# Attention and a dense layer on one core: query loads ahead of key copies, masks on VectorE

## The chip, the cores and the metric

The kernel runs on one core of a Trainium2 chip. A core has TensorE (matmuls; PE in the profile), VectorE (DVE), ScalarE (ACT), GpSimd (POOL) and SyncE (SP), each with a queue of instructions that it works off in order, and 16 DMA engines between HBM and the on-chip memory. DMAs are issued from the queues of SyncE and of POOL. The metric is device time of one execution in microseconds.

## The reference

Block-sparse attention, then a dense layer; 4 batches, 8 heads, 768 tokens, head size 64, blocks of 32 tokens:

```python
mask = np.abs(blk_i - blk_j) <= 1
mask = mask | (blk_i == 0) | (blk_j == 0) | (blk_i == n_blocks - 1) | (blk_j == n_blocks - 1)
for qb in range(n_blocks):
    for kb in sampled_blocks[qb]:                 # three random blocks for each query block
        mask[qb*32:(qb+1)*32, kb*32:(kb+1)*32] = True
scores = np.where(mask, scale * q @ k.T, -1e9)
attn = exp(scores - max) / (sum + 1e-9)
x = (attn @ v)                                    # to 3072 tokens x 512
h = x @ w_in                                      # 512 x 2048, weights given as float64
g = s * relu(h)**2 + b
return g @ w_out
```

Which blocks are sampled is known only at run time.

## The kernel before, in words

Attention is cut into slots. Four dense slots in each half of the batches handle the first and last query block, which see all keys. A sparse slot handles one query block of two batches: 256 score columns, made of window blocks, global blocks and three sampled blocks. There are 44 sparse slots; here they are counted from 0, so that slots 0, 1 and 2 are the first of three streams and use the query tiles qr_4s, qr_0s and qr_3s, one tile for four slots of a stream. Order at the start: four dense slots (qr_0d), then the sparse slots of the first half.

One sparse slot is this work. POOL copies its window keys and global keys out of the key tile kt into kk (lines 880 and 882), the last block (891), and three sampled blocks (893), whose numbers it holds in registers. TensorE makes the scores from kk and the query tile (943). VectorE adds the mask mt and takes the maximum (960), ScalarE takes the exponential (972), TensorE transposes (1000), VectorE and ScalarE copy the result to pt (1011, 1013), TensorE multiplies with window values vA and sampled values vB (1052), VectorE scales (1058), TensorE transposes back (1064), ScalarE copies (1069), SyncE spills to xd (1076). TensorE takes these in a written-out order: scores of slot i+2, value product of slot i, transposes of slot i+1, transposes back of slot i, scores of slot i+3, and so on. Sampled keys are held for four slots and sampled values for five, so POOL copies for a slot when the scores four slots before are done, and SyncE loads sampled values up to five slots ahead. Window values go into one of three rows of vA, free when the product three slots before is done.

At the start SyncE loads the sampled list (795), the keys of the first half in eight pieces (692), the first dense queries (706), global values (758, 760), window values (771) and, with registers that it loads from the tile packed (837), sampled values (865). VectorE makes packed from the list (801 and the helper line 100). POOL makes constants, then `sparse_sampled`, a chain of 17 small instructions that writes the mask mt (helper line 100), then loads the registers (837), then works on queries (706) and key copies.

Behind attention 256 us into the execution comes the dense layer, which TensorE fills nearly to the end; its weights are loaded and split during attention.

A planner sets the order on each engine: every operation has an engine, a cost, a priority (a due time in units of TensorE's work, smaller is earlier), and what it depends on (`deps`), follows (`order`, the start of another operation) or allocates. The planner issues the earliest startable operation in order of priority. The engines keep the order that comes out; on the chip only semaphores hold them. DMAs take turns in eight lanes for each issuing queue, so a DMA waits until the one eight before it has landed.

## Time and profile before

| | us |
|---|---|
| median of 3 runs (780.3 to 783.9) | 780.48 |
| profiled execution | 780.98 |
| its span | 779.2 |
| TensorE busy | 735.6 (94%) |
| VectorE busy | 579.0 (74%) |
| ScalarE busy | 472.1 (61%) |
| POOL busy | 240.1 (31%) |
| TensorE busy, 0 to 20 us | 16.43 |
| TensorE busy, 30 to 40 us | 6.34 |

The page has a row of busy time for each engine, the span in 40 slices, the DMA queues, the chain of work that ended last, and groups of instructions. The trace also answers with a timeline of one engine, with waits, and with the busy time in a given stretch. In a row of the timeline the first number is the start, the second the length, x the count, and in brackets stands the idle time before it with what ended it. "Issue" is time in which the engine waited for nothing that the profile shows; a register load is such time. Lines are those of the kernel before.

### The profile page before, as it was taken

To read this page: it belongs to the slowest core of one execution; us is meant where nothing else is said; L and a number is where in the kernel's file an instruction comes from. 1 tells how busy PE (TensorE), PEld (TensorE's weight loads), DVE (VectorE), ACT (ScalarE), POOL (GpSimd) and SP (SyncE) were. 2 spreads that over 40 slices of the span, in tenths; PEclk is the share of its full clock that TensorE was granted. 3 is DMA by queue.
4 is the path that set the end of the run, shared out by engine and by line. 5 is a ranking of instruction groups with operands and counts; after the bars stand their busy time and mean duration, and the time that the engine had idled before them with its cause. 6 is when DMAs were issued, how large, how long until landed. Compare 5 with 4: busy or idle time off the path is not lost.

```text
span 779.2 us, 21332 instructions
## 1 busy us (share of the span) xinstructions
PE 735.6 (94%) x8032; PEld 619.8 (80%) x8032; DVE 579.0 (74%) x1441; ACT 472.1 (61%) x1141; POOL 240.1 (31%) x390
## 2 busy tenths in 40 slices
PE   8799798988798999999889999999999999999997
PEld 6377675566576998998778899988888888988996
DVE  4657477878687699999897688687678678666652
ACT  4657475977687677778864344465544467445443
POOL 4746243524320232221022223222322233222321
PEclk9989999999899999999999999999999999999999
DMA  9988988856774544544623321225000022000002
GB/s 242 217 211 227 235 227 236 197 146 186 191 203 130 149 135 137 165 156 128 141 108 95 89 75 68 68 63 135 0 1 2 1 61 82 1 1 0 2 1 81
DMA packets 101110, 89.41 MB, mean 115 GB/s; under 512 B 50192, under 2 KB 79504, under 8 KB 101008
## 3 DMA queue, kind: packets, MB, share of 16 engines
q1 hardware_dynamic: 98704, 81.76, 38.2%
q0 software_dynamic: 2304, 6.29, 3.4%
q8 instruction: 63, 1.03, 0.6%
q14 instruction: 39, 0.32, 0.1%
HBM read 69.15 MB, written 14.68 MB: 108 GB/s over the span
## 4 chain that ended last, share of the span: by engine, by line
PE 79%; DVE 7%; ACT 4%; issue 4%; DMA 3%; POOL 1%; SPq 1%; POOLq 0%; ACTq 0%; DVEq 0%
PE m L611 19%; PE o L475 10%; PE o L476 10%; PE o L474 10%; PE s L943 6%; PE xs L1052 6%; PE t L1000 5%; PE h L432 3%; PE h L434 3%; PE h L433 3%; PE od L1042 2%; PE xs L1064 1%; DMA qr_3s<-in_q_dup_dram 1%; DMA xd<-xst 1%; DVE xp L595 1%
## 5 line engine op out<-in xcount | busy, mean ns | idle before, releaser
L453 POOL TENSOR_TENSOR hid<-hid,hid 128x384 fp32r<-128x384 f32 x120 | 132.3, 1103 | 400.5 <-ACT hid L629 249.0
L628 ACT ACTIVATE hid<-hid,sb_b,sb_s 128x384 f32<-128x384 f32 x96 | 68.0, 709 | 151.8 <-DVE hid L622 151.8
L972 ACT ACTIVATE ptile<-ptile,nm 128x256 f32<-128x256 f32 (+1 forms) x208 | 107.3, 518 | 43.2 <-DVE nm L960 42.8
L960 DVE CUSTOM_DVE_ANT_1 ptile<-s,mt 128x256 f32<-128x256 f32 x176 | 64.4, 421 | 34.7 <-PE s L943 33.6
L476 PE MATMUL o<-woutr,hid 128*128 128x512 f32 x168 | 66.5, 396 | 0.0
L475 PE MATMUL o<-woutr,hid 128*128 128x512 f32 x168 | 66.3, 395 | 0.0
L611 PE MATMUL m<-wout,win 128*128 128x384 f32 x264 | 62.7, 340 | 3.6 <-ACT hid L437 1.9
L474 PE MATMUL o<-woutr,hid 128*128 128x512 f32 x168 | 65.3, 389 | 0.0
L611 PE MATMUL m<-xp,wop 128*128 128x384 f32 x288 | 58.3, 337 | 0.0
L475 PE MATMUL o<-win,hid 128*128 128x512 f32 x144 | 56.8, 394 | 0.0
L622 DVE SCALAR_TENSOR_TENSOR hid<-hid 128x384 f32<-128x384 f32 x96 | 54.3, 566 | 3.3
L1052 PEld LDWEIGHTS xs<-vA,pt 128*32 128x32 f32 x1696 | 36.1, 113 | 26.0 <-issue 8.7
L611 PE MATMUL m<-xp,win 128*128 128x384 f32 x288 | 55.1, 338 | 1.4 <-DVE xp L595 0.7
L1000 PE MATMUL t<-ident,ptile 128*128 128x128 f32 x352 | 51.4, 289 | 3.6 <-issue 3.5
L611 PEld LDWEIGHTS m<-xp,win 128*128 128x128 f32 x288 | 51.0, 188 | 4.6 <-DVE xp L595 1.2
L1052 PE MATMUL xs<-vA,pt 128*32 128x64 f32 x1696 | 48.5, 228 | 6.2 <-issue 5.6
L629 ACT CAST hid<-hid 128x384 fp32r<-128x384 f32 x96 | 49.4, 515 | 7.2
L611 PEld LDWEIGHTS m<-xp,wop 128*128 128x128 f32 x288 | 51.5, 188 | 2.1
L611 PEld LDWEIGHTS m<-wout,win 128*128 128x128 f32 x264 | 47.3, 188 | 6.9 <-ACT hid L437 2.8
L882 POOL COPY kk<-kt 128x256 f32<-128x256 f32 (+2 forms) x46 | 20.5, 449 | 103.3 <-PE s L943 103.3
L476 PE MATMUL o<-win,hid 128*128 128x512 f32 x126 | 49.8, 395 | 0.0
L474 PE MATMUL o<-win,hid 128*128 128x512 f32 x126 | 49.2, 390 | 0.2
(187 smaller groups left out, 1843.3 us busy)
## 6 DMA issues: line engine op xcount, KB each, us to landing
vB<-in_v_dram SPq DMA_DIRECT2D x109, 128.0 KB, 3.9
vA<-in_v_dram SPq DMA_DIRECT2D x72, 128.0 KB, 4.1
raw_o<-in_w_out_dram SPq DMA_DIRECT2D x14, 512.0 KB, 3.3
raw_i<-in_w_in_dram SPq DMA_DIRECT2D x12, 512.0 KB, 3.8
xd<-xst SPq DMA_DIRECT2D x44, 128.0 KB, 3.8
out_dram<-ob SPq DMA_DIRECT2D x20, 256.0 KB, 2.0
sum<-xd SPq DMA_DIRECT2D x12, 384.0 KB, 4.4
kt<-in_k_blk_dram SPq DMA_DIRECT2D x8, 384.0 KB, 5.4
```

Source lines behind the costliest of these rows:

```text
L453: (eng or nc.vector).tensor_tensor(out=htile(5 + i % 3), in0=t, in1=gh.bitcast(F32), op=ALU.subtract)
L474: nc.tensor.matmul(acc, gh[:, tsl], wout(f, 0), start=first, stop=False)
L475: nc.tensor.matmul(acc, gh[:, tsl], wout(f, 1), start=False, stop=False)
L476: nc.tensor.matmul(acc, gl[:, tsl], wout(f, 0), start=False, stop=last)
L611: nc.tensor.matmul(to, w_, x_, start=(c == 0 and k == 0), stop=(c == 1 and k == 2))
L622: vec.scalar_tensor_tensor(out=t, in0=t, scalar=0.0, in1=t, op0=ALU.max, op1=ALU.mult)
L628: nc.scalar.activation(t, t, AF.Identity, bias=sb_b, scale=sb_s)
L629: nc.scalar.copy(gh, t)
L960: nc.vector.tensor_tensor_reduce(out=pt, in0=sp, in1=msk, scale=-scale, scalar=FMAX if g == 0 else nm[:, 0:1], op0=ALU.add, op1=ALU.min, a ...
L972: nc.scalar.activation(pt[:, :w], pt[:, :w], AF.Exp, bias=nms[n][:, last:last + 1], scale=-1.0, accum_out=dns[i][:, g, j:j + 1])
L1000: nc.tensor.transpose(tp[:, (2 * j + c) * P:(2 * j + c + 1) * P], src[:, c * P:(c + 1) * P], ident)
L1052: nc.tensor.matmul(xs[quads[pair]], pt[:, c, quads[pair]], vt[:, a, col:col + D], start=(j == 0 and c == 0), stop=(c == 1), tile_position= ...
```

## The change

Five edits. The mask chain goes from POOL to VectorE, behind the making of packed. The planner's priority of the query loads of the first three sparse query tiles is lowered by 8, they are asked for ahead of the slot's key copy instead of behind it, and they need only the register load ahead of them. Later sparse query loads are put behind the last sampled copy of the slot before, where they had to follow only the very first window copy. The first two loads of the first dense query tile get priority -27 and so go ahead of all keys. The priority of the register loads goes from -8.0 to -8.45, which on SyncE puts the load ahead of the first value loads.

```diff
-    "GK": 15.0, "GV": 13.0, "KL": 26.0, "K1": 9, "KA": 17.0, "QL": 18.0, "VL": 11.0, "DL": 12.0, "DE": 44.0, "SI": -30.0, "RS": -8.0, "MS2": -29.0,
+    "GK": 15.0, "GV": 13.0, "KL": 26.0, "K1": 9, "KA": 17.0, "QL": 18.0, "VL": 11.0, "DL": 12.0, "DE": 44.0, "SI": -30.0, "RS": -8.45, "MS2": -29.0,
...
-        o_ss = chain("g", nc.gpsimd, 270, T["MS2"], sparse_sampled, o_sb)
+        o_ss = chain("v", nc.vector, 220, T["MS2"], sparse_sampled, o_si)
...
-                if not dense:
-                    first_q = first_q or qk
+                if not dense:
+                    early_q.append(qk)
...
-                        pq = op("s" if dense else "g", 450 if dense else 700, max(u - T["QL"], -18.0 if dense else -4.5) + 0.01 * par + (9.5 * (u == 0) if dense else 0.02) * a,
+                        pq = op("s" if dense else "g", 450 if dense else 700, (-27.0 if u == 0 and a == 0 else max(u - T["QL"], -18.0 if dense else -4.5)) + 0.01 * par + (9.5 * (u == 0) if dense else 0.02) * a - 8.0 * (not dense and len(early_q) <= NST),
...
-                                order=[pq] if dense else [pq, o_rg if first_q in (None, qk) else first_pk], nbytes=131e3)
+                                order=[pq] if dense else [pq, o_rg if len(early_q) <= NST else last_pk], nbytes=131e3)
...
+                queries()
                 pk = op("g", 1900 if entire else 430, u - T["GK"], lambda i=i, w=entire: window_k(i, w),
-                        [*parts_of(e, blocks), *(prev[0] if prev else [])], alloc=new, use=[(f"kt{e}", e)] + ([] if first else [("kk", "kk")]), order=[pk])
+                        [*parts_of(e, blocks), *(prev[0] if prev else [])], alloc=new, use=[(f"kt{e}", e)] + ([] if first else [("kk", "kk")]), order=[pk] if pk else [pq])
                 s_deps.append(pk)
-                first_pk = first_pk or pk
-                queries()
...
+                last_pk = pk
```

POOL, behind its constants, before (iv, t_126 and mt belong to the mask, of whose 17 instructions the last two are shown; L837 is the register load, L706 the query loads, L880 to L893 the key copies of slot 0):

```order
L100 TENSOR_TENSOR iv<-iv,t_126 128x22
L100 TENSOR_SCALAR mt<-iv 128x22x3
L837 TENSOR_LOAD packed
L706 DMA qr_4s<-in_q_dup_dram 64x4x128 x4
L880 COPY kk<-kt_129 128x256
L882 COPY kk<-kt_129 128x512
L882 COPY kk<-kt_129 128x256
L891 COPY kk<-kt_129 128x256
```

and in the changed kernel, from the last constant on:

```order
L789 MEMSET mt 128x1
L837 TENSOR_LOAD packed
L706 DMA qr_4s<-in_q_dup_dram 64x4x128 x4
L706 DMA qr_0s<-in_q_dup_dram 64x4x128 x4
L706 DMA qr_3s<-in_q_dup_dram 64x4x128 x4
L880 COPY kk<-kt_137 128x256
L882 COPY kk<-kt_137 128x512
```

The mask is gone from here, and the second and third query sets, which stood behind the copies of slots 0 and 1, stand ahead of them. With its waits shown, the third set has one on the lanes of the first set. Farther on, the loads of qr_5s stood behind the copies of slots 5 and 6 and now stand behind those of slot 11; in the second half the first tile's loads move from behind slots 18 and 19 to behind slot 21.

SyncE at the start, before (sbi is the sampled list, kt the keys, qr_0d the dense queries, vA and vB values):

```order
L692 DMA kt_129<-in_k_blk_dram 128x6x128 x4
L706 DMA qr_0d<-in_q_edge_dram 64x4x128 x2
L692 DMA kt_129<-in_k_blk_dram 128x6x128 x4
L706 DMA qr_0d<-in_q_edge_dram 64x4x128 x2
L758 DMA vA<-in_v_dram 32x3x512 x2
L758 DMA vB<-in_v_dram 32x4x512 x2
L760 DMA vA<-in_v_dram 32x2x512
L771 DMA vA<-in_v_dram 64x2x512
L771 DMA vA<-in_v_dram 32x2x512
L837 TENSOR_LOAD packed
```

and in the changed kernel:

```order
L706 DMA qr_0d<-in_q_edge_dram 64x4x128 x2
L692 DMA kt_137<-in_k_blk_dram 128x6x128 x8
L706 DMA qr_0d<-in_q_edge_dram 64x4x128 x2
L837 TENSOR_LOAD packed
L758 DMA vA<-in_v_dram 32x3x512 x2
L758 DMA vB<-in_v_dram 32x4x512 x2
L760 DMA vA<-in_v_dram 32x2x512
L771 DMA vA<-in_v_dram 64x2x512
L771 DMA vA<-in_v_dram 32x2x512
```

The first half of the dense queries goes ahead of all keys, the second half stays behind them, and the register load goes ahead of the global and window values. On VectorE the 17 mask instructions stand between the making of packed and the first dense maximum. TensorE's and ScalarE's orders are the same as before.

More of the change, by code (lines that the diff above doesn't have):

```diff
@@ L1139 @@
         devs, drc, done, late, held, pav = {}, {}, {}, {}, set(), None
-        first_pk = first_q = pq = pvl = pvs = pk = o_m = o_e = o_rc = o_ev = None
+        early_q = []
+        last_pk = pq = pvl = pvs = pk = o_m = o_e = o_rc = o_ev = None
         spills, tensor, lqs, before, globs = {}, {}, {}, {}, []
@@ L1150, in queries @@
             def queries():
-                nonlocal pq, first_q
+                nonlocal pq
                 if qk in lqs:
```

## The prediction

> **What bounds the kernel now.** I read the chain of waits for the first 60 us, then the timelines of POOL, VectorE, TensorE and SyncE in that stretch, then the stages for DMA. Behind attention the same chain is TensorE work almost without a gap, in an order that the change leaves alone; so only the start matters. The chain of waits, 0 to 60 us (start, length, what):
>
> ```profile
> 11.38 5.27 issue
> 16.66 1.35 POOL qr_4s L706 x2
> ...
> 28.68 10.81 DMA qr_3s<-in_q_dup_dram
> ...
> 39.54 1.08 PE s L943 x8
> 40.62 1.86 PE xs L1052 x64
> 42.48 1.90 PE t L1000 x8
> ...
> 44.81 1.43 PE s L943 x32
> 46.24 1.03 PE xs L1052 x64
> ...
> 48.35 1.02 PE t L1000 x8
> ...
> 49.59 1.02 PE s L943 x32
> ...
> 54.99 0.91 PE xs L1052 x53
> ```
>
> POOL leads until 28.68: a register load, then query loads. Then one query load (qr_3s) takes 10.81 us to land, and TensorE sets the pace from 39.54 on. Work at 40.62 to 46.24 runs slower than the same work later (1.86 against 1.03, 1.90 against 1.02, 1.43 against 1.02). Now POOL, whose queue is in order:
>
> ```profile
> 10.93 0.46 POOL L100 TENSOR_SCALAR mt<-iv 128x66 f32<-128x66 f32 x1
> 16.66 2.70 POOL L706 DMA_DIRECT2D qr_4s<-in_q_dup_dram  x4 [5.27 <-issue]
> ...
> 26.87 2.43 POOL L706 DMA_DIRECT2D qr_3s<-in_q_dup_dram  x4
> ...
> 31.77 0.39 POOL L882 COPY kk<-kt 128x256 f32<-128x256 f32 x1
> ```
>
> The last mask instruction ends at 11.39; the register load is the 5.27 us behind it; only then are queries issued, the third set after the key copies of two slots. The copies of the first three slots begin when the first set is issued (16.66 + 2.70 = 19.36) and end at 31.77. What TensorE loses:
>
> ```profile
> 23.43 0.61 PE L998 MATMUL t<-ident,ptile 128*96 128x128 f32 x4 [0.21 <-DVE nm L960]
> 24.95 2.51 PE L943 MATMUL s<-kk,qr_4s 64*32 64x256 f32 x32 [0.91 <-DMA qr_4s<-in_q_dup_dram]
> ...
> 29.75 0.64 PE L998 MATMUL t<-ident,ptile 128*96 128x128 f32 x4 [0.84 <-ACT ptile L972]
> 30.32 1.07 PE L943 MATMUL s<-kk,qr_0s 64*32 64x256 f32 x24
> ...
> 32.29 1.09 PE L1000 MATMUL t<-ident,ptile 128*128 128x128 f32 x8
> 35.74 2.84 PE L943 MATMUL s<-kk,qr_3s 64*32 64x256 f32 x24 [2.36 <-DMA qr_3s<-in_q_dup_dram]
> ```
>
> Thirty-two score matmuls take 1.02 us when nothing is missing (49.59). Beyond that: before the first set 0.91, inside it 2.51 - 1.02 = 1.49, in the second (30.32 to 32.29) 0.95, before the third 2.36, inside it (35.74 to 40.62) 3.86. Sum 9.57 us. All of it is queries that are late.
>
> **The change part by part.** *Masks to VectorE.* VectorE was idle:
>
> ```profile
> 5.55 0.25 DVE L100 CAST packed<-cl 128x24 int32<-128x24 f32 x1
> 11.38 0.56 DVE L960 CUSTOM_DVE_ANT_0 ptile<-s,mz 128x384 f32<-128x384 f32 x1 [5.58 <-POOL mt L100]
> ```
>
> Seventeen small dependent instructions at 0.25 each (the cast's row) are 4.3 us; from 5.55 + 0.25 = 5.80 they end at 10.1, inside the 5.58 us gap. Cost 0. Without that cover they would push the first dense maximum back, up to 4.3. POOL's register load can start at 5.80 instead of 11.39: queries are issued from 5.80 + 5.27 = 11.07.
>
> *Three query sets in a row.* 2.70 + 2.43 + 2.43 (the second priced like the third): issue ends at 18.6 instead of 26.87 + 2.43 = 29.30. Twelve DMAs are now ahead of the first key copy, and the third set waits for lanes of the first, so it may stop POOL until pieces of the first have landed; behind it are the copies, and behind those the scores. The durations to landing (last column, us) of transfers issued at 12 to 20 and at 20 to 26:
>
> ```profile
> qr_4s<-in_q_dup_dram POOLq DMA_DIRECT2D x4, 128.0 KB, 8.1
> ...
> qr_0d<-in_q_edge_dram SPq DMA_DIRECT2D x1, 128.0 KB, 4.8
> ```
>
> ```profile
> q0 software_dynamic: 276, 0.77, 61.4%
> q1 hardware_dynamic: 331, 0.56, 42.7%
> ...
> vA<-in_v_dram SPq DMA_DIRECT2D x3, 128.0 KB, 7.2
> vA<-in_v_dram SPq DMA_DIRECT2D x1, 384.0 KB, 10.1
> ```
>
> With 8.1 to landing the third set goes out at 19.2 to 21.6, and the copies of slot 0 (2.6 us; 21.96 was when the second set followed them) end at 24.2 instead of 21.96, those of slot 2 at 29.2 (31.77 - 29.30 = 2.5 a slot); with 4.8 there is no such wait and they end at 21.2 and 26.2. The third set lands 8.1 to 10.81 behind an issue that ends between 18.6 and 21.6: 26.7 to 32.4. Without waits its scores would end at 40.62 - 9.57 = 31.05, so begin at 30.0; the worst case makes them late by 2.4. Gain at this point between 7.2 and 9.57; I take the middle, 8.4, since both ends come from rows equally near.
>
> [...]
>
> *Clock.* The slow stretch of 40.62 to 46.24 costs 0.83 + 0.88 + 0.41 = 2.1 us. It follows the idle 2.36 us and the broken third set; if these go, 2.1 is won, at worst 0. I take 2.1; the waits before it go. [...]
>
> *Dense queries ahead of keys.* First dense scores may start earlier, but VectorE, which started on them at 11.38, now has masks until 10.1: at most 1.3 us. The second half keeps its place behind all keys. I take 0.
>
> *SyncE's register load* now stands ahead of the first seven value loads:
>
> ```profile
> 15.13 1.30 SPq L771 DMA_DIRECT2D vA<-in_v_dram  x2
> 21.50 2.44 SPq L865 DMA_DIRECT2D vA<-in_v_dram  x3
> ...
> 42.33 0.33 SPq L771 DMA_DIRECT2D vA<-in_v_dram  x1
> ```
>
> The load, with what it waits for, is 21.50 - (15.13 + 1.30) = 5.07 us. The seven loads go out about 5 us later, the sampled values still near 21.5, landing by 21.50 + 2.44 + 7.2 = 31.1. The first attention product, won forward to 40.62 - 8.4 = 32.2, finds them. Cost 0; were they 10.1 in landing, 34.0, so 1.8.
>
> *Later query loads* stand up to six slots nearer to their use; qr_5s now follows the copies of slot 11:
>
> ```profile
> 62.67 0.40 POOL L882 COPY kk<-kt 128x256 f32<-128x256 f32 x1 [1.93 <-PE s L943]
> ```
>
> These are slot 11's copies, released by the scores of slot 7. With three more copies of 0.39 they end at 64.2; 2.43 for issue and 8.1 to land give 74.7 in the old time. Slot 12's scores follow the transposes at 74.65 (quoted below) by more than a slot, and a slot is 4.8 us (44.81 to 49.59). Cover nearly 5 us, cost 0; with 10.81 to land still 2.
>
> *What is late next.* Won so far: 8.4 + 2.1 = 10.5 at 46 us. The window values of slot 3 are the first load that cannot move with it. It went out at 42.33, behind six sampled loads ending at 39.1 that only the landing rate holds; so now at about 39.5 and landing 4.8 to 10.1 later, 44.3 to 49.6; with 7.2, 46.7. Its product is wanted at 54.99 - 10.5 = 44.5. Lost: 0 to 5.1, I take 2.2. Then DMA as a whole (us, engines' busy us, clock, DMA share, GB/s):
>
> ```profile
> 40.00:80.00 40.00, 37.29 (x1101) 28.20 (x1097) 26.44 (x116) 27.52 (x96) 21.40 (x52) 0.93 0.83 221
> 80.00:120.00 40.00, 37.00 (x1083) 28.11 (x1077) 25.29 (x106) 24.48 (x83) 14.96 (x39) 0.96 0.90 232
> 70.00:90.00 20.00, 15.33 (x438) 11.88 (x424) 10.72 (x48) 10.63 (x38) 10.49 (x24) 0.91 0.96 241
> ```
>
> To keep a lead the same bytes must move in less time. Taking 0.96, the fullest stage, as all that can be had, 40 x 0.13 + 40 x 0.06 = 7.6 us are free up to 120 us: the remaining 8.3 shrinks to 7.6. And fuller DMA has a price seen in that stage:
>
> ```profile
> 74.65 1.03 PE t L1000 x8
> ...
> 77.43 2.14 issue
> 79.57 1.35 PE xs L1052 x45
> 80.93 1.90 PE t L1000 x8
> ```
>
> TensorE stops in the middle of a burst, waiting for nothing that the profile shows, then runs slow: 2.14 + (1.35 - 45/64 x 1.03 = 0.63) + 0.88 = 3.65 us. I charge half of one more such stop, 1.8. 7.6 - 1.8 = **5.8 us**. The profiled execution took 780.98 (span 779.2, 1.8 around it): 775.2. It lies 0.5 above the median of 780.48, so I predict **774.7**.
>
> **Rivals.** *All of it survives:* sampled values are loaded up to five slots ahead, so a lag of DMA may never reach TensorE, and no product waits for values between 42 and 77 us now. Against: window loads have less lead. 780.48 - 10.5 = 770.0. *Nearly all is given back:* window values land at 10.1 (lost 5.1) and the clock is not won (2.1), the half stop stays: 10.5 - 5.1 - 2.1 - 1.8 = 1.5, 779.0. For it: DMA at 0.96; against: only 0.83 in 40 to 80. That the query loads are not earlier at all would end there too; the register load that held them has its masks gone, so I give it little. *Slower:* DMA that is full from 20 to 120 us stops TensorE in mid-burst more often, each 3.65. Two more eat the 7.6; from the third it is slower, 783.8, with four 787.5. For it: such a stop came where the share was highest (0.96); against: the chain shows none of that length before 77 us, in a stage with 0.83.
>
> **Chances.** Forecast (4 to 8 won) 0.47, all survives 0.17, given back 0.25, slower than before 0.11. A difference under 0.5% (3.9 us) can't be told from none. Faster by more: 0.44 + 0.17 = 0.61; slower by more (over 784.4, four stops): 0.07; the rest 0.32. The range runs from 769.5 (all survives, and a little of the dense start) to 781.5 (beyond the given-back case; the stops are left out). The likeliest case alone: 772.5 to 777.
>
> **What would show it.** POOL's register load right behind 5.8, three query sets issued by 18.6 to 21.6, the copies of three slots by 29; score matmuls of 1.02 to 1.5 us with no wait for queries; the first attention product at 31 to 34 instead of 40.62. I am wrong if waits for vA or vB appear between 35 and 60 us, if the dense part starts later than 11.38, or if long stops in mid-burst multiply before 120 us. The lead where the dense layer begins should equal the difference of the times.

## The result and the profile after

The changed kernel takes 783.19 us (median of 22 runs, 777.72 to 785.96), the kernel before beside it 780.35 us (22 runs). The ratio is 1.0033 with a 95% interval of 1.0017 to 1.0049: 2.6 us longer, where 5.8 us less was forecast. That lies inside the half per cent which the prediction calls no change, and outside its range. The profiled execution took 783.0 us, with a span of 781.2 (before: 780.98 and 779.2).

GpSimd does what was forecast. Its timeline after the change (start, length, engine, line, operation; in brackets how long the engine was idle and what ended it):

```profile
11.62 2.60 POOL L706 DMA_DIRECT2D qr_4s<-in_q_dup_dram  x4 [9.38 <-DVE nm L960]
14.21 2.44 POOL L706 DMA_DIRECT2D qr_0s<-in_q_dup_dram  x4
16.93 0.62 POOL L706 DMA_DIRECT2D qr_3s<-in_q_dup_dram  x1 [0.28 <-DMA qr_4s<-in_q_dup_dram]
18.17 0.62 POOL L706 DMA_DIRECT2D qr_3s<-in_q_dup_dram  x1 [0.62 <-DMA qr_4s<-in_q_dup_dram]
19.42 1.23 POOL L706 DMA_DIRECT2D qr_3s<-in_q_dup_dram  x2 [0.63 <-DMA qr_4s<-in_q_dup_dram]
20.64 0.41 POOL L880 COPY kk<-kt 128x256 f32<-128x256 f32 x1
...
27.21 1.08 POOL L893 COPY kk<-kt 128x256 f32 x3
```

The queries go out from 11.62 (before: 16.66), the third set in three pieces that wait for lanes of the first, and then the key copies of three slots follow without a pause, from 20.64 to 28.29 (before: 19.35 to beyond 34, with query loads of 2.43 us between the slots). VectorE in the same stretch:

```profile
5.72 0.19 DVE L100 TENSOR_SCALAR iv<-sbf 128x66 f32<-128x66 f32 x1
...
9.42 0.20 DVE L100 TENSOR_SCALAR mt<-iv 128x66 f32<-128x66 f32 x1
10.24 0.56 DVE L960 CUSTOM_DVE_ANT_0 ptile<-s,mz 128x384 f32<-128x384 f32 x1 [0.62 <-PE s L921]
...
25.55 2.42 DVE L981 SCALAR_TENSOR_TENSOR rc<-dn 128x2 f32<-128x2 f32 x1
28.00 0.17 DVE L984 RECIPROCAL rc<-rc 128x2 f32<-128x2 f32 x1
...
33.73 0.15 DVE L981 SCALAR_TENSOR_TENSOR rc<-dn 128x2 f32<-128x2 f32 x1
```

The masks end at 9.62 and the first dense maximum starts at 10.24, earlier than before (11.38). But L981, the sum of two columns ahead of the reciprocal, takes 2.42 us on a tile of 128 x 2, where it takes 0.15 at 33.73. It ends at 27.97, while the last of GpSimd's copies runs (27.90 to 28.30). TensorE then:

```profile
17.47 0.86 PE L921 MATMUL s<-kt,qr_0d 64*64 64x384 f32 x4 [1.56 <-DMA qr_0d<-in_q_edge_dram]
...
20.97 3.13 PE L998 MATMUL t<-ident,ptile 128*96 128x128 f32 x16
...
29.37 0.61 PE L998 MATMUL t<-ident,ptile 128*96 128x128 f32 x4 [2.38 <-DVE nm L960]
29.91 1.99 PE L943 MATMUL s<-kk,qr_4s 64*32 64x256 f32 x32
...
37.87 1.09 PE L943 MATMUL s<-kk,qr_3s 64*32 64x256 f32 x32
38.99 1.10 PE L1052 MATMUL xs<-vA,pt 128*32 128x64 f32 x55
41.96 0.35 PE L1052 MATMUL xs<-vA,pt 128*32 128x64 f32 x9 [1.87 <-issue]
```

No score matmul of a sparse slot waits for queries any more. In their place stand a wait for the second half of the dense queries (1.56), the 2.38 us behind L981, and a stop of 1.87 us inside the first attention product, in which TensorE waits for nothing that the profile shows. Scores of slot 0 start at 29.91 instead of 24.95; the first attention product starts 1.63 us earlier than before (38.99 instead of 40.62), not 8.4.

The second query half is late, landing 6.11 us after issue (before: 5.02): in 14 to 18 us the two queues share the DMA engines (queue, packets, MB, share of the engines' time; first the change, then before), where before the hardware queue had them to itself:

```profile
q1 hardware_dynamic: 890, 0.43, 57.6%
q0 software_dynamic: 179, 0.52, 57.5%
```

```profile
q1 hardware_dynamic: 859, 0.90, 110.8%
```

Lastly the stages. Columns: busy us (and instructions) of TensorE, its weight loads, VectorE, ScalarE, GpSimd; granted clock; DMA share; GB/s. After:

```profile
30.00:60.00 30.00, 26.51 (x682) 19.45 (x682) 20.44 (x91) 20.90 (x73) 10.42 (x29) 0.94 0.81 203
60.00:90.00 30.00, 24.52 (x697) 18.30 (x697) 17.04 (x74) 18.06 (x63) 15.75 (x36) 0.94 1.00 249
90.00:118.00 28.00, 27.00 (x813) 20.55 (x812) 19.58 (x83) 19.42 (x67) 9.08 (x25) 1.00 0.62 177
```

and before:

```profile
30.00:60.00 30.00, 25.77 (x628) 17.30 (x626) 16.76 (x73) 16.83 (x59) 13.63 (x37) 0.83 0.87 207
60.00:90.00 30.00, 25.33 (x724) 19.44 (x713) 18.14 (x80) 18.92 (x68) 14.10 (x35) 0.94 0.90 236
90.00:118.00 28.00, 27.53 (x822) 20.57 (x824) 19.80 (x84) 20.62 (x72) 12.55 (x33) 1.00 0.87 228
```

The clock of 30 to 60 us rose from 0.83 to 0.94 and TensorE did 54 matmuls more there; from 60 to 90, with a DMA share of 1.00 in place of 0.90, it did 27 fewer.

To follow a lead through the kernel I read, from TensorE's timeline, when the scores of each sparse slot start. Slot 21 is the last of the first half, slot 43 the last of all; the rest of the kernel takes 534.6 to 536.3 us from there in all fifteen profiles of kernels that do all the work, so the time is decided by slot 43.

| kernel (one profile each), start in us | slot 0 | slot 3 | slot 9 | slot 19 | slot 22 | slot 31 | slot 43 | span |
|---|---|---|---|---|---|---|---|---|
| before | 24.9 | 44.7 | 69.2 | 113.7 | 149.7 | 188.6 | 243.8 | 779.2 |
| before, second profile | 24.8 | 43.6 | 68.5 | 113.7 | 152.9 | 188.3 | 242.3 | 778.2 |
| the change | 29.9 | 43.5 | 67.9 | 114.9 | 154.7 | 189.8 | 246.1 | 781.2 |
| old order of the later queries | 29.1 | 44.1 | 69.1 | 113.6 | 154.0 | 190.8 | 246.3 | 782.0 |
| query order alone | 26.2 | 41.4 | 65.1 | 113.5 | 155.7 | 190.5 | 244.2 | 780.5 |
| masks alone | 24.4 | 39.1 | 65.3 | 111.6 | 150.9 | 188.0 | 243.1 | 778.5 |
| one-input reduction | 24.9 | 38.6 | 64.0 | 111.7 | 153.0 | 188.7 | 243.4 | 779.1 |
| the same, second profile | 24.5 | 35.2 | 65.3 | 117.5 | 156.4 | 191.1 | 246.2 | 781.3 |
| second query half | 25.6 | 38.6 | 63.7 | 110.4 | 153.4 | 188.3 | 246.7 | 781.3 |
| the same, second profile | 29.3 | 42.2 | 66.6 | 114.2 | 154.2 | 189.9 | 246.2 | 782.0 |
| both repairs | 23.4 | 35.3 | 64.2 | 110.0 | 149.5 | 185.3 | 237.3 | 772.1 |
| the same, second profile | 23.4 | 36.9 | 65.0 | 113.3 | 152.9 | 187.9 | 245.1 | 781.1 |

The two profiles of the kernel before differ by 3.2 us at slot 22. So a difference of a few microseconds behind slot 19 in one profile is not a property of a kernel, and the verdicts below rest on the times, not on that part of the table.

### The profile page after: what moved, and what is told of

Read it like the earlier page. It is cut to its first block, busy times and chain, and to the rows that moved or that the text cites. A ratio compares the mean times of both kernels' runs of the same rounds, so it can differ in the third digit from the quotient of the medians.

```text
span 781.2 us, 21336 instructions
## 1 busy us (share of the span) xinstructions
PE 735.0 (94%) x8032; PEld 621.9 (80%) x8032; DVE 583.0 (75%) x1458; ACT 472.3 (60%) x1141; POOL 235.4 (30%) x373
## 3 DMA queue, kind: packets, MB, share of 16 engines
q0 software_dynamic: 2304, 6.29, 3.4%
q8 instruction: 63, 1.03, 0.6%
## 4 chain that ended last, share of the span: by engine, by line
PE 78%; DVE 8%; ACT 4%; DMA 4%; issue 3%; SPq 2%; ACTq 0%; DVEq 0%
PE m L611 19%; PE o L475 10%; PE o L476 10%; PE o L474 10%; PE xs L1052 6%; PE s L943 6%; PE t L1000 5%; PE h L432 3%; PE h L434 3%; PE h L433 3%; DMA vA<-in_v_dram 2%; PE od L1042 2%; PE xs L1064 1%; DVE ptile L960 1%; PE t L998 1%
## 5 line engine op out<-in xcount | busy, mean ns | idle before, releaser
L972 ACT ACTIVATE ptile<-ptile,nm 128x256 f32<-128x256 f32 (+1 forms) x208 | 107.2, 518 | 44.7 <-DVE nm L960 44.4
L960 DVE CUSTOM_DVE_ANT_1 ptile<-s,mt 128x256 f32<-128x256 f32 x176 | 64.2, 421 | 27.3 <-PE s L943 26.8
L474 PE MATMUL o<-woutr,hid 128*128 128x512 f32 x168 | 65.3, 389 | 0.0
L475 PE MATMUL o<-win,hid 128*128 128x512 f32 x144 | 56.8, 394 | 0.0
L476 PE MATMUL o<-win,hid 128*128 128x512 f32 x126 | 49.8, 395 | 0.0
L893 POOL COPY kk<-kt 128x256 f32 x132 | 49.6, 414 | 0.0
```

The costliest lines, as they stand in the source:

```text
L474: nc.tensor.matmul(acc, gh[:, tsl], wout(f, 0), start=first, stop=False)
L475: nc.tensor.matmul(acc, gh[:, tsl], wout(f, 1), start=False, stop=False)
L476: nc.tensor.matmul(acc, gl[:, tsl], wout(f, 0), start=False, stop=last)
L893: nc.gpsimd.tensor_copy(flat(kg[:, a:a + 1]), flat(kts[e][:, bass.ds(j, 1)]))
L960: nc.vector.tensor_tensor_reduce(out=pt, in0=sp, in1=msk, scale=-scale, scalar=FMAX if g == 0 else nm[:, 0:1], op0=ALU.add, op1=ALU.min, a ...
L972: nc.scalar.activation(pt[:, :w], pt[:, :w], AF.Exp, bias=nms[n][:, last:last + 1], scale=-1.0, accum_out=dns[i][:, g, j:j + 1])
```

## The experiments

Two theories stood against each other first. "Start": the change lost what it should have won within its first 30 us, to VectorE's L981 and to the late second query half. "Order" and "DMA": the start is good enough, and the loss comes later, from the new order of the later query loads or from the full DMA stage. Four kernels ask it. Long lines of an edit are shown with only the part that changes.

**The old rule for the later queries.** The change, with the query loads behind the first three slots ordered as before:

```diff
-    order=[pq] if dense else [pq, o_rg if len(early_q) <= NST else last_pk]
+    order=[pq] if dense else [pq, o_rg if len(early_q) <= NST else first_pk]
...
-                last_pk = pk
+                first_pk = first_pk or s_deps[0]
```

> The changed kernel, but the later query loads keep the order rule of the kernel before (behind the first window copy, not behind the last sampled copy). The first three query sets, the masks and the dense queries stay as changed, so SyncE's queue between 95 and 115 us and POOL's later loads are those of before. Theory 'order' (the loss is made at 117 to 137 us, where SyncE's order moved: the lag against before grows from 1.5 us at slot 20 to 4.5 at slot 21): about 3 us less than the changed kernel, 780 or below, with the lag at slot 21 no larger than at slot 20. Theory 'start' (the loss is made before 31 us): same as the changed kernel, 783. Theory 'DMA' (the full stage at 60 to 95 us takes what is won before it): 783.

Measured: 783.5 us, ratio 1.0031 (1.0002 to 1.0060), as slow as the change. The order of the later loads is not what costs.

**The reduction with one input tile.**

```diff
-    nc.vector.scalar_tensor_tensor(out=rc, in0=dn[:, 0, :nu], scalar=1e-9, in1=dn[:, 1, :nu], op0=ALU.add, op1=ALU.add)
+    nc.vector.tensor_reduce(out=rc, in_=dn[:, :, :nu].rearrange("p g j -> p j g"), axis=mybir.AxisListType.X, op=ALU.add)
```

> The changed kernel, but the sum of the two halves of a dense denominator (line 981) is a reduction over one input instead of an operation with two inputs; the 1e-9 that it added to a sum of at least 1 is left out. Theory 'start': this instruction took 2.42 us at 25.55 because POOL was copying without a pause until 28.24; with one input it takes under 0.4, the scores of slot 0 begin 2.2 us earlier (27.7 instead of 29.91), and the time falls to 781. Rival within it: the instruction waits for something else, takes 2.4 again, and nothing moves. Theory 'DMA': the scores come earlier, the time stays 783. Theory 'order': 783.

Measured: 781.09 us, ratio 1.0000 (0.9973 to 1.0026). VectorE and TensorE's first attention product in its profile:

```profile
22.81 0.16 DVE L981 TENSOR_REDUCE rc<-dn 128x2 f32<-128x4 f32 x1
```

```profile
33.07 1.15 PE L1052 MATMUL xs<-vA,pt 128*32 128x64 f32 x55
```

L981 takes 0.16 us while GpSimd copies as before, and the first attention product starts at 33.07, 7.55 us ahead of the kernel before. The time returns to that of the kernel before, not below it.

**The second query half between the key halves.**

```diff
-    (-27.0 if u == 0 and a == 0 else max(u - T["QL"], -18.0 if dense else -4.5))
+    ((-27.0 if a == 0 else -19.0) if u == 0 else max(u - T["QL"], -18.0 if dense else -4.5))
```

> The changed kernel, but the second half of the first dense queries goes between the two halves of the keys instead of behind both. Theory 'start': TensorE's wait of 1.56 us for these queries (17.47) and VectorE's behind it shrink to under 0.6 us, the scores of slot 0 begin 1 to 1.5 us earlier, 782. Rival: the last keys are then late by as much, nothing moves, 783. Theories 'DMA' and 'order': 783.

Measured: 782.06 us, ratio 1.0025 (1.0001 to 1.0048). TensorE's wait of 1.56 us for the queries is gone, and a wait for the last keys has come in its place: 1.55 us here, 0.72 in the second run below. So the rival in the expectation is right in part. Slot 3 starts at 38.6, and L981 takes 0.80 us at most. That was this execution's luck: its first turn came 2.3 us into the copies, and in the second run it came 2.1 us into them and was held.

**The masks alone**, on the kernel before:

```diff
-        o_ss = chain("g", nc.gpsimd, 270, T["MS2"], sparse_sampled, o_sb)
+        o_ss = chain("v", nc.vector, 220, T["MS2"], sparse_sampled, o_si)
```

> The kernel before, with the one edit that the masks are made by VectorE. Query loads, copies and SyncE's queue keep the order of before, so POOL's register load and all behind it begin 5.5 us earlier (query sets at 11.1, 16.4 and 21.3), and key copies are broken up by query loads. Theory 'start': no long chain of copies, no late dense queries; scores of slot 2 are done 4 to 6 us earlier than before (35 to 37 instead of 40.62), 776 to 778. Theory 'DMA': scores of slot 2 are earlier, but the lead is gone by slot 12 and the time is 780. Theory 'order': SyncE's order is that of before, so 780 or less.

Measured: 780.58 us, ratio 0.9998 (0.9974 to 1.0021). In its profile the masks alone bring slot 3 5.6 us forward, since the register load and all behind it on GpSimd begin earlier; nothing of it is left in the time.

The 776 to 778 that theory "start" expected here is missed. So "start" names a part of the loss at most, and the runs raise the second question: why does a start that is 5 us better win nothing? Four more kernels ask it, all but the last on the change with both repairs.

**Both repairs.** The last edits of the reduction and of the query half together, run twice.

> The changed kernel with both repairs of its start: the second dense query half between the two key halves, and the reduction ahead of the reciprocal with one input tile (without the added 1e-9). Both theories expect the first slots early: slots 3 to 9 at least 5.5 us ahead of the kernel before. Theory 'start' expects the total to keep half of that, 777.5 or less. Theory 'crossing' (the lead is lost between 65 and 150 us, to a full DMA stage and to SyncE's queue of weight loads and late values, whatever the start was) expects slot 21 to be behind the kernel before, by 1 to 4 us, and 780 to 782.5.

Measured: 778.72 us, ratio 0.9990 (0.9961 to 1.0019). The profiled execution was the fastest of eleven, so it was run again:

> The kernel with both repairs a second time, for a closer interval. If its lead at slot 43 of 6.5 us in the first profile was that execution's alone, this profile has -3 to +3 there and a median of 779 to 781; if it is the kernel's, the lead is there again and the median is 776 to 779.

Measured: 781.34 us, ratio 0.9990 (0.9962 to 1.0018); slot 43 at 245.1, behind the kernel before. The 6.5 us in the first profile were that execution's. The repaired change is as fast as the kernel before, and the 777.5 or less of theory "start" is missed here too.

**Weight loads later in SyncE's queue**, on both repairs:

```diff
-    "WE": -90.0
+    "WE": -78.0
```

> As the kernel with both repairs, with the weight loads let into SyncE's order 12 steps of the clock of the order later (-78 in place of -90), so that the first stands 21 rows further down, behind the values of the second half's first slots. If the weight loads in SyncE's queue cost the lead at the crossing, slot 21 is now at or ahead of the kernel before, and the time is 2 to 5 us under the kernel with both repairs. If the DMA engines as a whole are what is short there, slot 21 stays 2 to 5 us behind and the time is within 1 us. If the second half is bound by the weight splitting on VectorE and ScalarE, slot 21 is ahead but the time is within 1 us, or 1 to 4 us longer, since the splitting starts later.

Measured: 781.43 us, ratio 1.0000 (0.9969 to 1.0030). Not the weight loads, or not by their place alone.

**Keys of the second half two slots later**, on both repairs:

```diff
-    "K1": 9
+    "K1": 11
```

> As the kernel with both repairs, with the key pieces of the second half loaded two slots later (11 in place of 9). If the full DMA stage between 60 and 95 us is what takes the lead ahead of slot 13, the DMA share there falls under 0.9, the stops in it are shorter, slots 11 to 13 are 4 us or more ahead of the kernel before, and the total is 1 to 3 us under the kernel with both repairs, as far as slots 20 to 22 don't take it. If only the crossing takes it, slots 11 to 13 move by under 2 us, slots 20 to 22 are 2 to 5 us behind or worse since keys arrive later, and the time is the same or up to 3 us longer.

Measured: 781.85 us, ratio 0.9994 (0.9952 to 1.0036). The expected fall of the DMA share from 60 to 90 us didn't come: it was 0.98, perhaps since SyncE went on with what stood behind the keys. So this run says nothing on the full stage.

**The query order alone**, the change with its masks back on GpSimd:

```diff
-        o_ss = chain("v", nc.vector, 220, T["MS2"], sparse_sampled, o_si)
+        o_ss = chain("g", nc.gpsimd, 270, T["MS2"], sparse_sampled, o_sb)
```

> The change without its masks on VectorE: the query order alone. GpSimd does the 12 mask operations again ahead of its register load, so the sparse queries are issued some 5 us later than with the change (at about 16.6) and the copies start behind them, at about 26, and run to 34. Both theories expect the first slots late: slots 0 to 2 at 2 to 8 us behind the kernel before. Theory 'start' expects a total of 784 to 788, worse than the change. Theory 'crossing' expects the lag to be taken up between slots 22 and 31 and the total within 1 us of the change, 782 to 784.

Measured: 783.38 us, ratio 1.0038 (1.0011 to 1.0064). GpSimd's copies run from 23.51 without a pause until beyond 34, and L981 is held again. Yet slots 0 and 1 start only 1.3 and 0.9 us behind the kernel before, where both theories expected 2 to 8, slot 3 starts 3.3 us ahead of it, and the 784 to 788 of theory "start" is missed too. At 80.68 us TensorE waits 6.29 us for window values. The row of L981 over the first 250 us in this kernel, then in the one with the old rule for later queries (shortest, median and longest, in ns):

```profile
L981 DVE SCALAR_TENSOR_TENSOR rc<-dn x8: 141/151/4459, 21.0 to 161.8; 128x2 f32<-128x2 f32 x8
```

```profile
L981 DVE SCALAR_TENSOR_TENSOR rc<-dn x8: 140/149/4397, 22.3 to 160.1; 128x2 f32<-128x2 f32 x8
```

Three kernels with the change's query order and the reduction of two inputs, three holds (2.42, 4.40, 4.46 us), three ratios of 1.0031 to 1.0038.

**Half of the values left out.** Theory "pace of transfers": a lead at the start is lost because the attention stage runs at the pace of its transfers. From the tenth sparse slot on, window and sampled values are loaded for one of the two batch rows only:

```diff
-            rr = runs(k, entire)
+            rr, few = runs(k, entire), slice(0, 1 if 12 < i else 2)
...
-            nc.sync.dma_start(out=window_values(r)[p * BLK:(p + n) * BLK], in_=block_rows(e, j, n))
+            nc.sync.dma_start(out=window_values(r)[p * BLK:(p + n) * BLK, few], in_=block_rows(e, j, n)[:, few])
...
-            nc.sync.dma_start(out=vt[a * BLK:(a + 1) * BLK], in_=src[bass.ds(j, 1)].rearrange("o e a d -> (o e) a d"))
+            nc.sync.dma_start(out=vt[a * BLK:(a + 1) * BLK, few], in_=src[bass.ds(j, 1)].rearrange("o e a d -> (o e) a d")[:, few])
```

With both repairs, all the way:

> The kernel with both repairs, whose window and sampled values are loaded from the tenth sparse slot on for one of a slot's two batch rows only (the other keeps old values: half of these bytes are left out, and the output is not the reference's). Order and instructions of the compute engines stay. Theory 'DMA' (what takes the lead between 60 and 150 us is the full DMA stage, through stops of TensorE ahead of fetched code and through late values) expects TensorE's idle time from 30 to 115 us to fall from 10.5 to 7 or less, slot 19 at least 7 us ahead of the kernel before (the kernel with both repairs: 3.6), no wait for values at 115 to 150, slot 21 at least 5 ahead, and a time of 774 or less. Theory 'compute' (VectorE and ScalarE pace the stretch behind 110 us, whatever arrives) expects slots 21 to 31 within 2 us of the kernel with both repairs and 777 to 780.

Measured: 767.75 us, ratio 0.9822 (0.9772 to 0.9872). Bytes moved from 30 to 250 us, with both repairs and then with these halves left out:

```profile
DMA packets 39941, 45.33 MB, mean 206 GB/s; under 512 B 14373, under 2 KB 25893, under 8 KB 39879
```

```profile
DMA packets 36935, 36.48 MB, mean 166 GB/s; under 512 B 15503, under 2 KB 27620, under 8 KB 36873
```

A fifth of the bytes less takes about 14 us off in this run. But the path expected for it isn't there: TensorE's idle time from 30 to 115 us stayed at 10.1 us and the lead at slot 19 was 5.9, not 7. The same up to the end of the first half alone (`12 < i < 30` in the edit):

> As the one before, but only up to the end of the first half (sparse slots 9 to 21; half of the value bytes of these is left out, the output is not the reference's). Theory 'DMA' expects slots 19 and 21 as far ahead as there, and what is left at slot 43 and at the end within 2 us of that kernel, since behind 150 us the DMA share is only 0.65. If the second half's own loads cost something too, it ends 2 us or more behind that kernel.

Measured: 773.93 us, ratio 0.9915 (0.9882 to 0.9947): the bytes cost time in both halves. Its profile drew a late slot 3 (38.9), so the slot times expected of it can't be read from it.

**The kernel before, a second profile.**

> The kernel before a second time, one look. If the slot times of one profile stand for the kernel, slots 0 to 9 come within 0.5 us of the first profile, and slots 13 to 43 within 1.5 us; if executions differ by which stops fall into them, slots 20 to 22 differ by 2 us or more.

Measured: 780.01 us. Slots 0 to 2 come within 0.24 us; slot 4 differs by 1.57, slot 21 by 3.41 and slot 43 by 1.54. Executions differ by more than the question needs.

Now the decisive comparison, on one chip: if transfers take the lead away, then with transfers relaxed the three starts must show.

> The kernel before with the same halves of the value bytes left out from the tenth sparse slot on (the output is not the reference's). The repaired change with these left out took 767.75. Theory 'pace of transfers': the lead of the repaired start is lost because transfers pace slots 3 to 31, so with them relaxed it comes through; the kernel before without these bytes takes 771 to 775, at least 3 us more than the repaired change without them. Rival 'start is worth nothing': 766 to 769, the same as the repaired change without them.

> The changed kernel with the same halves left out (the output is not the reference's). Its slots 0 to 2 are 2 to 5 us behind the kernel before and slot 3 1 us ahead. 'Pace of transfers': with less to transfer the late first slots are made up by slot 9 as they were, and it ends within 2 us of the kernel before without these bytes, or some 5 us behind the repaired change without them. If the loss of 2.6 us comes from somewhere behind the start, it shows here too: 2 to 3 us over the kernel before without these bytes.

> The repaired change with the same halves left out, a second time, beside the two others on one chip. 766 to 770 by both theories; the theories differ in its distance from the two others.

Measured: the kernel before 770.33 us, ratio 0.9882 (0.9855 to 0.9909); the change 770.4, 0.9880 (0.9848 to 0.9912); both repairs 768.95, 0.9863 (0.9833 to 0.9893). The expected 3 us between repaired and before are 1.4, and the intervals overlap: relaxing the value transfers brings all three forward by 9 to 11 us and doesn't let the starts' difference through. "Pace of transfers" is right in that bytes cost time here, and fails as the reason for the lost lead. In the profile of the repaired kernel the lead was 6.8 us at slot 19 and 2.8 at slot 20 against the kernel before with the same bytes. The chain of waits there:

```profile
101.88 3.87 DMA vA<-in_v_dram
...
109.01 3.28 DMA vA<-in_v_dram
```

Values were issued at 109.01, and at 112.21 in the kernel before with half the bytes: SyncE's queue was 3.2 us ahead where TensorE was 6.8 ahead. With it went the rest.

**The one-input reduction without the change**, on the kernel before.

> The kernel before with the reduction of one input tile ahead of the reciprocal (without the added 1e-9, the change's reduction untouched otherwise). Before, that instruction took 0.77 us at most, so if it is only the change's unbroken chain of GpSimd copies that made it 2.42 us, nothing moves: 779.5 to 781.5, ratio within 0.0015 of 1. If the form with one input is cheaper everywhere, the time falls here too, by 1.5 to 3 us.

Measured: 780.35 us, ratio 0.9998 (0.9971 to 1.0025). Where query loads stand between the copies, the form with one input changes nothing in the time.

**Each repair a second time**, since the first intervals didn't part them.

> The change with the one-input reduction alone, a second time (without the added 1e-9). If the stalled reduction is what the change loses by: 780 to 781.5 where the kernel before has 780.3 (ratio 0.998 to 1.0015). If its first result was chance: 782 to 784 (1.002 to 1.005).

> The change with the second dense query half back between the key halves, a second time; the reduction has two inputs, but stood at 0.80 us at most in its first profile, since its turn came ahead of most of the copies. If the stall is what costs, whatever removes it: ratio 0.998 to 1.0015. If the repair of the query half alone doesn't give the loss back: 1.002 to 1.005.

Measured: the one-input reduction 779.68 us, ratio 0.9979 (0.9950 to 1.0008); the query half 783.85, ratio 1.0030 (1.0003 to 1.0057). And the second profile of the query half shows the hold:

```profile
21.67 5.22 DVE L981 SCALAR_TENSOR_TENSOR rc<-dn 128x2 f32<-128x2 f32 x1
26.92 0.17 DVE L984 RECIPROCAL rc<-rc 128x2 f32<-128x2 f32 x1
```

That settles which of the two repairs counts: moving the query half does not keep L981 from being held and doesn't give the loss back; the reduction with one input does both.

## Why the prediction was wrong

**Masks to VectorE, cost 0**: right. They ran from 5.72 to 9.62 (forecast 5.80 to 10.1), and alone they change nothing in the time (0.9998).

**Three query sets in a row, 8.4 us won at the first attention product**: wrong, 1.63. The working was right on GpSimd: queries from 11.62 (11.07), the third set's issue ended at 20.65 (18.6 to 21.6), the copies at 28.3 (26.2 to 29.2), no score waits for queries. The step that failed is that the early queries would carry through to the product. What it overlooked is that semaphores are not all that holds an engine: L981, 0.15 us long at 33.73, took 2.42 us at 25.55 while GpSimd copied. Before, it came just ahead of a query load, and its second turn among the copies of the next set:

```profile
21.80 0.23 DVE L981 SCALAR_TENSOR_TENSOR rc<-dn 128x2 f32<-128x2 f32 x1
...
29.72 0.77 DVE L981 SCALAR_TENSOR_TENSOR rc<-dn 128x2 f32<-128x2 f32 x1
```

In the changed order, without 2.43 us of query issue between one slot's copies and the next, the first turn falls into 7.6 us of copies, and it was held until the last of them. With the one-input reduction the product started 7.55 us earlier, inside the forecast's 7.2 to 9.57.

The reduction also decides whether the change is slower at all: in the change's query order, with the reduction of two inputs, ratios were 1.0025 to 1.0038 in five comparisons (the change, the old rule, the query order alone, the query half twice); with one input they were 0.9979 to 1.0000 in six (that reduction twice, both repairs twice, and both repairs with later weights or keys). That the one-input reduction gives the 2.6 us back is shown. That it does so by ending the hold is argued, and three things stand against a simple path from the hold to the time. The profile of the query half with a hold of only 0.80 us took 783.08 us all the same. With half the value bytes the change had a hold of 4.39 us and took what the kernel before took (0.9880 and 0.9882), within 0.4%. And the loss doesn't show at the start: averaged over the five profiles in the change's order with two inputs (all value bytes), slot 3 starts 1.1 us ahead of the average of the kernel before (three profiles) and the masks alone, slot 19 starts 0.7 ahead (both within the standard error of 1.4 to 1.7), slot 22 starts 2.7 behind and slot 43 2.7 behind (standard errors 0.9 and 0.6). The 2.6 us show up between slots 19 and 22, where the second half of the batches begins, and what the reduction at 25 us has to do with that stays open.

**Dense queries ahead of keys, 0**: the second half doesn't merely keep its place. It landed 6.11 us after issue and TensorE waited 1.56 for it. In 14 to 18 us, while it was under way, SyncE's queue had 57.6% of the engines' time and GpSimd's, with the early queries, 57.5%, where SyncE's had all (110.8%) before. The share of the late half in the time couldn't be told from none: repaired alone, 1.0025 and 1.0030; beside the other repair, 0.9990 twice.

**Clock, 2.1 us**: the slow stretch at 40 to 46 us is gone (clock 0.94 in place of 0.83 for 30 to 60 us), and two slow ones have come, behind the wait for the dense queries (1.56 us) and behind L981 (2.38): the clock is 0.66 from 19 to 24 us, where sixteen transposes took 3.13 us, and 0.66 from 29 to 34. So the slow stretch moved with the waits, and the 2.1 us were not clear profit.

**SyncE's register load and later query loads, 0**: the load by luck, the queries right. No wait for values came between 35 and 60 us in the change, but its first product was late. In six of the seven profiles with all value bytes whose first product came at 31 to 34 us (those with the one-input reduction, and the first of the query half), it stopped 0.7 to 1.9 us for window or sampled values, about the 1.8 that the prediction named as the worst case. The old order of the later queries is worth nothing (1.0031).

**What is late next, 2.2 + 0.7 + 1.8 lost of 10.5**: wrong, the second step that failed. The start was won by the repaired kernels, and all of it was lost. Over the fifteen profiles of kernels that do all the work, slot 3 starts at 34.6 to 45.0 us; a least-squares line gives only 0.26 us at slot 43 for one at slot 3, with a correlation of 0.39. In place of the three terms the runs showed:

- *A stop that the query wait had hidden.* In the first attention products TensorE stops in mid-burst in every one of the sixteen profiles with a short query wait or none in slot 2, save the query order alone (0.23 us): 1.1 to 3.4 us in the sum of two places. In the four profiles of the kernel before (two of its own, one with the one-input reduction, one with half the value bytes), where the wait for the third query set comes just ahead, there is none at all. The chain of the one-input kernel, then that of both repairs:

```profile
33.07 1.15 PE xs L1052 x55
34.22 2.20 issue
...
42.11 1.06 issue
```

```profile
37.56 0.49 PE od L1042 x11
38.06 2.81 issue
40.87 1.15 PE od L1042 x21
```

The places in the program are the same each time (55 matmuls into slot 0's product, 11 into a dense one), only the length varies. So of the 3.86 us at the third set that the sum counted as won, 1.1 to 3.4 came back as a stop. The last section has what the traces show of these stops and of the wait that hid one. The prediction had seen such stops, at 77 us, and charged half of one.

- *Other idle time in the full DMA stage.* The sum took a DMA share of 0.96 as all that can be had; the change had 1.00 from 60 to 90 us and did less work there. From 30 to 115 us TensorE's idle time before its matmuls (gaps from 0.15 us) was 9.3 and 10.4 us in the two profiles of the kernel before, 3.3 to 3.7 of it for queries and 5.7 and 7.1 in such stops; in the change 9.9, of which 9.1 in stops; with both repairs 10.5 and 12.1, where 6.1 of the second are waits for window values. The waits removed were replaced almost one for one. Single profiles scatter (9.1 and 14.0 with the one-input reduction alone, 12.9 in the kernel before with it), but on average the sum doesn't fall.

- *Window values, but not at slot 3.* In the four profiles with the query order of before and all value bytes, TensorE waits 0 to 2.0 us for values from 28 to 250 us; in the eleven others 0.5 to 10.6. Beside the first product, these waits stand at 77 to 81 us (2.4 to 6.3 us in four profiles) and at 117 to 129 us (0.2 to 4.8 us, in ten). So the load that the prediction feared is one of the takers, farther on than it looked.

- *A queue that isn't early.* In the kernels with the one-input reduction slot 3 starts 6 to 10 us ahead of the first profile of the kernel before and slot 19 at best 3.6, and on average the rest goes between there and slot 43. SyncE gives its transfers out in order, and its place moves less than TensorE's (3.2 against 6.8 with half the value bytes). With all bytes, five window loads in a row went out 3.6, 2.4, 0.6 and 1.5 us ahead and 0.1 behind in the first profile of both repairs, from 98.3 to 124.6 us. This is shown for these places; that it accounts for all that is lost behind slot 19 is not. Neither moving the weight loads nor the keys in its queue, nor halving the value bytes, let the lead through. One rival is left untested: SyncE itself is busy issuing transfers for 47 to 51 of the 78 us from 42 to 120 in these kernels, and 54 with half the value bytes, which left the number of transfers as it was. Whether its own pace carries the stage, no run here asks.

**The sign that the prediction named** held: the lead where the dense layer begins equals the difference of the times (slot 43 2.3 us later, span 2.0 longer). Of the rivals, "nearly all is given back" was nearest in kind: it had 0.25 and expected window values at slot 3 to be the cause, while the held reduction, the stops and later window values were. "Slower" came at 783.19, near the price of its third stop (783.8). Its mechanism is there in part, 9.1 us of stops from 30 to 115 us in place of 5.7 and 7.1, but the kernels with one input have such stops too (5.8 to 13.2 us in their six profiles with all value bytes) and are not slower.

## What to carry to other kernels

Before moving a block of work ahead of another on an in-order queue, ask what the gap that it leaves behind was good for: here the query loads had stood between the key copies, where VectorE's small sum took 0.77 us at most, against 2.42 without them, and the wait for the queries had hidden TensorE's own stop (none before, 1.87 us in the change). A saving at the start of a long pipelined stage is worth what reaches the end of the stage; check by shifting the start in existing variants and reading where the shift is gone, rather than by subtracting the next two or three known waits. And when two profiles of one kernel differ by 3 us in the middle, only repeated times decide.

## What the runs showed of the hardware

A VectorE instruction with two SBUF inputs, 128 x 2 elements and 0.15 us long, was held for 2.4 to 5.2 us while GpSimd ran copies back to back (three in 1.08 us). In the change (2.42 us) and in the second profile of the query half (5.22) it ended 0.1 us behind the start of the last of them. The same sum with one input took 0.16 us at most under the same copies. In six profiles with the change's query order and two inputs it was held in five times over 2 us and once for 0.80. The maxima ahead of it (L960), which take one PSUM and one SBUF tile, and the reciprocal behind it, which takes one SBUF tile, weren't held: in the change the maximum at 25.04 took 0.56 us under copies, as at 10.24 without any, and the reciprocal took 0.17 at 28.00 while the last copy ran. In the change L981 waited until six of GpSimd's copies had ended, in that second profile through more. The rows show how long it was held and beside what; what holds it isn't shown. It isn't held each time: in the kernel before, L981 also met copies, at 29.72 to 31.62, and took 0.22 to 0.77 us. What lets it through there, and in the one profile with 0.80 us, wasn't found.

TensorE's stops in mid-burst stand at fixed places of the program and differ in length with the execution: behind 31 scores of one slot 0.4 to 3.9 us, behind 19 matmuls of another's product 1.0 to 3.4, wherever they are seen. The profile of the change has a queue for instructions:

```profile
q8 instruction: 63, 1.03, 0.6%
```

1.03 MB in 63 packets is 16 KB each. From 20 to 250 us the twenty profiles hold 198 stops of 0.15 us or more in which TensorE waits for nothing that the profile shows. Numbered along TensorE's queue (matmuls, weight loads, semaphore instructions), all 198 stand a multiple of 256 instructions apart, to within one; one packet for 256 instructions would be 64 bytes each. Of the 88 that last 1 us or more, each ends 1.2 to 1.7 us behind the end of a packet on this queue. The profiles of the kernel before and of the change alone hold 23 of the stops, and 10 of the long ones, which end 1.27 to 1.69 us behind a packet. So I read the stops as waits for the next packet of instructions; no row names them so.

By the same reading a wait for data can hide one. In the kernel before, the packet ahead of that place in the first attention product, 55 matmuls in, ran from 36.35 to 37.67 us, while TensorE stood waiting for the third query set, and there was no stop. In the change it ran from 39.30 to 40.52, when the product was already at work, and the matmuls went on at 41.96. And the next packet came later in the full DMA stage: in the change, after the places at 74.6 and 81.4 us it began only 4.0 us later, in the stage with a DMA share of 1.00, and TensorE stopped 2.58 and 1.13 us for it; after those from 97 to 110 us, in the stage with 0.62, it began 1.2 to 1.7 us later, and the stops were 0.2 us at most.
